# A sliding-window attention and gated-MLP kernel: the shape of its warm-up matmuls, the token parts of its first two tiles, and the places of its value-product runs

## Chip, cores and metric

The kernel runs on one core of a Trainium2 chip. The metric is the device time of one launch in microseconds. For the kernel before, three runs gave 557.01, 557.45 and 558.83 us, so the median is 557.45 us. One more run, with the profiler on, took 558.06 us; every duration in this document that comes from a row of the profile is from that run.

## What is computed

All matrices are bfloat16; there are 2048 tokens of 576 features.

```
xn = layernorm(x)                       # per token, no scale or shift
q, k, v = split(xn @ wqkv)              # 32 heads of 18
p = softmax(q k^T / sqrt(18))           # causal, a window of 256 tokens
s = concat(p v) @ wo
h = sigmoid(xn @ w_gate) * (xn @ w_up)  # 4608 wide
out = x + s * silu(h @ w_down)
```

## The kernel before

**Tiles.** The tokens are taken in four chunks of 512, each in four blocks of 128. The contraction over 576 features is five steps: four of 128 rows and one of 64 rows that is kept twice. `pair` (L119) issues every large matmul as two, on rows 0 to 63 and 64 to 127 of TensorE, which run beside each other. One such pair is four instructions of TensorE: two weight loads and two matmuls. A gate or up product of one 128-wide tile of the MLP is two such turns, `gate_up` (L991) with half 0 and half 1, of 512 tokens each; there are 36 tiles per chunk, then the down product `down` (L1075) with matmuls 288 wide.

**Order.** Nothing is ordered by hand. `build_graph` makes operations with estimates, priorities and dependences, and `schedule` (L1165) places them one after the other on a modelled clock, with attention work (scores, value products, output projection) laid between the MLP's tiles. `emit` then writes each engine's list with semaphore waits. A change in one place so moves the order of everything behind it.

**Value-product runs.** `build_pv` (L828) makes the products of the exponentials with the values for 16 heads at a time: two runs in each chunk, eight in all. A run is 128 small matmuls in the first chunk and 192 in the later ones, with as many weight loads, so 256 or 384 instructions that follow each other (row L854 of the profile). `schedule` does not start run number r before TensorE's list is at least `RUN_AT[r]` instructions long (L43, L1202). `at` counts weight loads, matmuls and an estimate of the waiting instructions.

**Start.** Layer norm of the first chunk runs block by block: statistics on VectorE (block 2 on ScalarE), the power by GpSimd (L555, L641), the scaling on VectorE (`ln:ap`, L563), the transposition on TensorE (`tr`, L650, four times two per block), the copy out of PSUM (`xe`, L631; ScalarE, for block 3 VectorE). The 64 rows that are kept twice are made apart: four small scalings on VectorE (`ln:dup`, L579, priority `DUP_PRIO`), one transposition for all blocks (`tr:two`) and one copy by ScalarE (`xe:two`). The first two MLP tiles (`NEARLY`) do not wait for all 512 tokens: `PARTS` (L76) cuts each turn over the four 128-row steps into token ranges, so that a range starts when its blocks' copies are done; `last_rows` (L1012) adds the fifth step for all tokens. Until the first block is there, `warm` (L496) issues matmuls of zeros: `NWARM` pairs, 43 before the first transposition and 10 behind it.

Of the kernel before, what the change touches and what calls it, by code (L numbers as in the profile page):

```python
# [12 lines left out]
P = 128  # L13
# [26 lines left out]
OENG = ("SP", "POOL")  # L40
PV_ORDER = (0, 5, -4, -3, -2, -1, 1, 2, 3, 4, 6, 7)
TURN_NS = 265.0
RUN_AT = (2138, 3723, 5614, 7169, 9467, 10942, 13309, 14840)  # L43
BINS = (((-4, 0, 1), (1, 1, 5), (6, 6, 2)),
        ((-2, 0, 3), (3, 3, 5)),
        ((0, 0, 5), (5, 5, 3)),
# [20 lines left out]
STATS_ACT = (2,)  # L67
APPLY_ACT = ()
ORDER = (("ln:ve:1", "ln:ap:0"), ("ln:ve:3", "ln:ap:2"), ("ln:am", "ln:rs:1"), ("ln:ve:3", "ln:dup:0"), ("ln:ve:3", "ln:dup:1"))
DUP_PRIO = 30  # L70
XE_ENG = ("ACT", "ACT", "ACT", "DVE", "ACT")
NWARM = (43, 10)
NEARLY = 2
FIRST_SLACK_NS = (-800.0, -1500.0)
BUSY_SLACK_NS = 1500.0
PARTS = (((0, 1), (1, 2), (2, 3), (3, 4)),) * NEARLY  # L76
NQK = 5

DMA_ISSUE_NS = {"SP": 640.0, "POOL": 520.0, "ACT": 650.0}
# [39 lines left out]
def pair(eng, outs, lhs, rhs, start, stop, swap=0, parts=False):  # L119
    res = None  # L120
    for i in range(2):
        t = i ^ swap
        res = eng.matmul(outs[i], lhs(ROWS[t], i), rhs(ROWS[t], i), start=start, stop=stop, tile_position=(64 * t, 0),  # L123
                         skip_group_check=parts)
    return res
# [137 lines left out]
class Builder:  # L263
# [17 lines left out]
    def op(self, eng, est, fn, name="", deps=(), prio=3, nbytes=0, odeps=(), acq=None, ni=0):  # L281
        o = Op(eng, est, fn, name, deps, prio, nbytes, odeps, acq)
        o.ni = ni
        assert ni or eng != "PE", name
        o.cidx = len(self.ops)
        self.ops.append(o)
        for d in o.deps:
            d.succs.append(o)
        for d in o.odeps:
            d.succs.append(o)  # L290
        return o
# [162 lines left out]
    def build_consts(self):  # L454
        op = self.op
        o1 = op("POOL", 200, lambda e: e.memset(self.ident[:, :], 0.0), "init:ident1", prio=0)
        o2 = op("POOL", 200, lambda e: e.affine_select(
            self.ident[:, :], self.ident[:, :], pattern=[[1, SW]], compare_op=ALU.not_equal, fill=1.0, base=0,
            channel_multiplier=-1), "init:ident2", deps=[o1], prio=0)
        self.op_ident = op("POOL", 200, lambda e: e.affine_select(  # L460
            self.ident[:, :], self.ident[:, :], pattern=[[1, SW]], compare_op=ALU.not_equal, fill=1.0, base=SW,
            channel_multiplier=-1), "init:ident3", deps=[o2], prio=0)
        zero = self.hT[:, 0, 0:P]
        z = op("DVE", 920, lambda e: e.memset(zero, 0.0), "init:zero", prio=0)
        self.op_negh = op("DVE", 60, lambda e: e.memset(self.neghalf[:, :], -0.5), "init:neghalf", prio=0)
        self.op_tab = op("ACT", 1500, lambda e: e.activation(self.tring[:, 0, 0:1], zero[:, 0:1], ACTF.Exp), "init:tab",
                         deps=[z], prio=0)
        self.warm_h = self.pool_f.hold()
        self.warm_src = zero
        self.warm(NWARM[0], z, None, 107)  # L470

    def load_wq(self, c, gi):
        sw, dw = self.r_wq.produce()
# [19 lines left out]
            o.slack = 5000.0 if c == 0 and name == "wv" else 2500.0  # L493
        return ds

    def warm(self, n, dep, before, est):  # L496
        h, zero = self.warm_h, self.warm_src

        def f_warm(eng):
            return pair(eng, self.halves(h, P), lambda r, t: zero[r, :],  # L500
                        lambda r, t: zero[r, :], True, True)
        for i in range(n):
            w = self.op("PE", est, f_warm, f"warm:{i}", deps=[dep], prio=4, acq=None if before else h, odeps=[before], ni=4)
            w.filler = h
            h.release(w)
            before = w

    def build_attn_consts(self):
        op = self.op
# [21 lines left out]
    def build_ln(self, c):  # L531
# [3 lines left out]
        for i in range(BPC):  # L535
# [40 lines left out]
            else:  # L576
                def f_two(e, mean=mean, rstd=rstd, x_in=x_in, i=i, op0=ALU.add if on_act else ALU.subtract):
                    row, col = x_in.ap
                    return e.tensor_scalar(self.xn2[:, i, :].rearrange("p (a c) -> p a c", a=2),  # L579
                                           bass.AP(x_in.tensor, x_in.offset, [row, (0, 2), (1, RD)]), mean, rstd, op0, ALU.mult)  # L580
                dup = op("DVE", 220, f_two, f"ln:dup:{st}", deps=[rs, ag], prio=DUP_PRIO)
                self.ln_dups.append(dup)
                self.r_st.release(ss, dup)
            self.r_st.release(ss, ap)
            if c:
                fl = self.flip(self.xnT[:, xs, :, i * P:(i + 1) * P], self.xnr[:, sn, :], f"flip:x:{st}", ("fx", xs, i),
                               deps=[dup, war], prio=2)
# [3 lines left out]
            h = self.pool_s.hold()  # L591
# [3 lines left out]
            tr = op("PE", (KB - 1) * 29.5, f_tr, f"tr:{st}", deps=[ap, self.op_ident, war], prio=0, acq=h, ni=4 * (KB - 1))  # L595
            self.r_xn.release(sn, tr)
            if i == 0:
                self.warm(NWARM[1], None, tr, 80)

            def f_xe(e, h=h, i=i):  # L600
                dst = self.xnT[:, xs, 1:KB, i * P:(i + 1) * P].rearrange("p k (t c) -> p t k c", t=2)
# [1 line left out]
            eng = XE_ENG[i]  # L603
            n = (KB - 1) * P
# [337 lines left out]
    def build_ffn(self, c):  # L942
# [48 lines left out]
        def gate_up(ft, h, half, acq, part=None, deps=(), behind=()):  # L991
            sw, fc = slots[ft // WG], slice((ft % WG) * P, (ft % WG + 1) * P)
            b0, b1 = (0, BPC) if part is None else PARTS[ft][part]
            t0, n = b0 * P, (b1 - b0) * P
            xin = (self.op_xnT[c] if part is None else self.op_x0)[b0:b1]

            def lhs(r, t, k):
                return self.wgs[r, sw, k - 1, t, fc] if k else self.wgr[r, rslots[ft // (2 * WG)], ft % (2 * WG) * P:(ft % (2 * WG) + 1) * P]

            def f(eng):  # L1000
                outs = [bank(h, w)[:, t0:t0 + n] for w in range(2)]
                if part is None:
                    return turn(eng, outs, lhs, lambda r, t, k: x_in[r, k, t0:t0 + n], half)
                return early_turn(eng, outs, lhs, lambda r, t, k: x_in[r, k, t0:t0 + n], half, part == 0)
            steps = len(BLOCKS[half] if part is None else BLOCKS[0])
            o = op("PE", steps * mm_ns(n), f, f"f1{half}:{c}:{ft}", deps=[xin, wops[ft // WG][0:1 + half if part is None else 1], deps],
                   prio=3 if part is None else 1, odeps=chain[half] if part is None else list(behind), acq=acq, ni=4 * steps)
            chain[half] = [o] if part is None else chain[half] + [o]
            self.ffn_last = o
            return o  # L1010
# [26 lines left out]
        if early:  # L1037
# [3 lines left out]
            for ft, h in enumerate(hs):  # L1041
                u = None
                for part in range(len(PARTS[ft])):
                    lo = gate_up(ft, h, 0, None if part else h, part, [u])
                    if ft == early - 1 and part == len(PARTS[ft]) - 1:
                        ahead = self.pool_f.hold()
# [118 lines left out]
    def schedule(self):  # L1165
# [19 lines left out]
        while nsched < len(ops):  # L1185
            best = None
            for e in ENGS:
# [10 lines left out]
                for o in cand:  # L1198
                    if e == "PE" and nxt is not None and o is not nxt:
                        continue  # L1200
                    st = max(free[e], ready_t[o.cidx])
                    if o.run and at < RUN_AT[runs]:  # L1202
                        continue
# [178 lines left out]
```

## Time and profile before

| | us |
|---|---|
| median of three runs | 557.45 |
| profiled run, whole | 558.06 |
| its span, first to last instruction | 556.8 |
| TensorE busy in it | 550.4 |
| VectorE, ScalarE, GpSimd busy | 324.5, 271.2, 208.6 |
| DMA, mean rate over the span | 136 GB/s |
| DMA, rate in the first 30 us | 237 GB/s |

A row of the timeline has the start in us, the time from the first start to the last end in us, the engine, the line, the operation, output and inputs with their shapes, and the count; brackets hold the idle time of the engine before it and what ended it. A matmul's end is modelled, and matmuls are pipelined: a matmul of 288 columns has a duration of 283 ns, yet a pair of them follows the last pair after some 119 ns. "Issue" is idle time for which the profile shows no semaphore. PEld are TensorE's weight loads. Waiting instructions are not counted in the views.

### The profile page before, as it was taken

How to read it: one execution, taken by the hardware profiler on the slowest of the kernel's cores; microseconds unless marked ns; L12 is line 12 of the kernel's file. 1: busy time of each engine (PE TensorE's matmuls, PEld its weight loads, DVE VectorE, ACT ScalarE, POOL GpSimd, SP SyncE). 2: the span in 40 equal slices, each digit the busy share in tenths (PEclk: the TensorE clock that was granted, in tenths of full speed). 3: DMA queues.
4: the chain of work that ended last, by engine and by line, in shares of the span. 5: the costliest groups of instructions: out<-in, count | busy, mean ns of one | idle time of the engine just before them, and what ended most of it. 6: DMA issues, size and time to landing. Idle time of an engine off the chain costs nothing.

```text
span 556.8 us, 19393 instructions
## 1 busy us (share of the span) xinstructions
PE 550.4 (99%) x8330; PEld 356.3 (64%) x8330; DVE 324.5 (58%) x782; ACT 271.2 (49%) x380; POOL 208.6 (37%) x360
## 2 busy tenths in 40 slices
PE   7999999999999999999999999999999999999998
PEld 7454445777756664468997555556778554445787
DVE  4467667756766558647546558556545477556211
ACT  4245563442565646653456626662556336762121
POOL 5634343846360333643730506542633305300300
PEclk9999999999999999999999999999999999999999
DMA  8999999442166673661153744754132246540010
GB/s 221 258 271 218 273 229 259 115 105 42 37 191 192 170 202 102 194 152 31 41 136 93 204 142 112 206 154 119 32 102 61 82 129 177 166 134 5 22 44 25
DMA packets 141213, 75.87 MB, mean 136 GB/s; under 512 B 43676, under 2 KB 139260, under 8 KB 141128
## 3 DMA queue, kind: packets, MB, share of 16 engines
q1 hardware_dynamic: 133704, 68.71, 46.6%
q0 software_dynamic: 7424, 5.92, 4.0%
q8 instruction: 66, 1.08, 0.8%
q14 instruction: 19, 0.16, 0.1%
HBM read 63.18 MB, written 2.36 MB: 118 GB/s over the span
## 4 chain that ended last, share of the span: by engine, by line
PE 98%; DMA 1%; issue 0%; SPq 0%; DVE 0%; ACT 0%
PE ps L123 95%; PE ps L854 3%; DMA wgs<-in_B_w_up_dram 1%; SPq L294 0%; PE ps L650 0%; ACT thf L1139 0%; DVE thf L1141 0%; DVE xf L1144 0%
## 5 line engine op out<-in xcount | busy, mean ns | idle before, releaser
L123 PE MATMUL ps<-xnT,wgs 64*128 64x512 bf16 (+1 forms) x2400 | 284.1, 368 | 0.4 <-DMA wgs<-in_B_w_up_dram 0.4
L804 ACT ACTIVATE expr<-ps 128x1024 bf16<-128x1024 f32 (+4 forms) x160 | 154.9, 968 | 77.5 <-PE ps L123 76.0
L123 PEld LDWEIGHTS ps<-xnT,wgs 64*128 64x128 bf16 x2400 | 119.8, 94 | 106.3 <-ACT xnT L631 0.5
L123 PE MATMUL ps<-wd_sb,hT 64*128 64x288 bf16 (+2 forms) x2448 | 155.9, 276 | 1.0 <-issue 0.8
L1025 ACT ACTIVATE tring<-ps 128x512 bf16<-128x512 f32 x144 | 86.2, 599 | 128.3 <-PE ps L123 127.4
L1028 DVE SCALAR_TENSOR_TENSOR hT<-tring,ps 128x512 bf16<-128x512 bf16 x144 | 98.7, 685 | 83.5 <-ACT tring L1025 81.5
L294 POOL DMA_DIRECT2D qk<-qd x160 | 82.7, 523 | 155.0 <-PE ps L123 148.5
L123 PEld LDWEIGHTS ps<-wd_sb,hT 64*128 64x128 bf16 x2448 | 117.8, 94 | 26.1 <-issue 1.6
L817 DVE TENSOR_TENSOR expr<-expr,mask 128x128 bf16<-128x128 bf16 (+2 forms) x240 | 63.9, 294 | 70.6 <-ACT expr L804 69.3
L294 POOL DMA_DIRECT2D oT<-o2T x72 | 36.8, 518 | 115.3 <-DVE o2T L890 71.6
L768 POOL TENSOR_SCALAR kx<-kprev,small 128x256 bf16<-128x256 bf16 x64 | 60.3, 952 | 5.6 <-PE ps L123 4.7
L123 PE MATMUL ps<-qk,kx 64*128 64x320 bf16 (+1 forms) x704 | 61.0, 254 | 0.0
L123 PE MATMUL ps<-xnT,wgr 64*128 64x512 bf16 x288 | 55.7, 376 | 0.0
L123 PEld LDWEIGHTS ps<-qk,kx 64*128 64x128 bf16 x704 | 34.7, 94 | 23.7
L123 PE MATMUL ps<-xnT,wqg 64*128 64x512 bf16 (+1 forms) x320 | 38.0, 355 | 0.0
L689 DVE CAST qd<-ps 128x1024 bf16<-128x1024 f32 (+1 forms) x20 | 22.3, 1115 | 7.7 <-PE ps L123 7.7
L123 PEld LDWEIGHTS ps<-xnT,wgr 64*128 64x128 bf16 x288 | 15.1, 94 | 15.8
L768 DVE TENSOR_SCALAR kx<-qk,small 128x512 bf16<-128x512 bf16 x64 | 21.7, 365 | 5.8 <-PE ps L123 5.5
L890 DVE STREAM_TRANSPOSE o2T<-o 128x512 bf16<-128x512 bf16 x32 | 22.6, 706 | 1.6 <-DMA oT<-o2T 1.1
L123 PEld LDWEIGHTS ps<-xnT,wqg 64*128 64x128 bf16 x320 | 15.9, 94 | 10.6 <-issue 0.4
L882 DVE STREAM_TRANSPOSE ot<-ps 128x512 f32<-128x512 f32 x32 | 20.1, 684 | 3.9 <-PE ps L854 3.9
L1141 DVE TENSOR_TENSOR thf<-thf,s_attn 128x576 bf16<-128x576 bf16 (+2 forms) x5 | 2.0, 398 | 31.4 <-ACT thf L1139 18.6
(71 smaller groups left out, 300.9 us busy)
## 6 DMA issues: line engine op xcount, KB each, us to landing
wgs<-in_B_w_gate_dram SPq DMA_DIRECT2D x72, 256.0 KB, 3.6
wgs<-in_B_w_up_dram SPq DMA_DIRECT2D x72, 256.0 KB, 4.1
wd_sb<-in_B_w_down_dram SPq DMA_DIRECT2D x9, 576.0 KB, 6.0
wqg<-in_A_wqkv_dram SPq DMA_DIRECT2D x32, 128.0 KB, 3.5
qk<-qd POOLq DMA_DIRECT2D x100, 36.0 KB, 2.4
wgr<-in_B_w_gate_dram SPq DMA_DIRECT2D x36, 64.0 KB, 2.5
wgr<-in_B_w_up_dram SPq DMA_DIRECT2D x36, 64.0 KB, 2.5
wvo<-in_A_wqkv_dram SPq DMA_DIRECT2D x4, 576.0 KB, 4.3
```

The costliest lines, as they stand in the source:

```text
L123: res = eng.matmul(outs[i], lhs(ROWS[t], i), rhs(ROWS[t], i), start=start, stop=stop, tile_position=(64 * t, 0), skip_group_check=parts)
L294: o = self.op(eng, DMA_ISSUE_NS[eng], lambda e: e.dma_start(dst, src), name, deps, prio, nbytes=nbytes)
L689: return eng.tensor_copy(dst, self.both(h, n))
L768: return e.tensor_scalar(self.kx[:, sx, pos:pos + n_ // SW, t, :], src.rearrange("p (s k) -> p s k", k=SW), self.half[:, t:t + 1], None, A ...
L804: return eng.activation(self.expr[:, se, :, lo * SW:NT], self.both(h, NT)[:, :, lo * SW:NT], ACTF.Exp, scale=SM_SCALE)
L817: return eng.tensor_tensor(e_, e_, m_, ALU.mult)
L854: res = eng.matmul(outs[i][p0:p0 + VH, cols], self.v_aug[ROWS[i], o:o + VH], self.expr[ROWS[i], se, t, cols], start=m == 0, stop=m == len( ...
L882: return e.transpose(self.ot1[:, p1, :], self.halves(hp, NT, un)[i])
L890: t2 = op("DVE", dve_ns(NT), lambda e, p2=p2, p3=p3: e.transpose(self.o2T[:, p3, :], self.o2[:, p2, :]), f"ot2:{c}:{pr}:{i}", deps=[on, d3 ...
L1025: th = op("ACT", act_ns(NT), lambda e: e.activation(self.tring[:, st, :], bank(h, 0), ACTF.Tanh, scale=0.5), f"th:{c}:{ft}", deps=[pg, dt_ ...
L1028: mu = op("DVE", dve_ns(NT), lambda e: e.scalar_tensor_tensor(self.hT[:, ft, :], self.tring[:, st, :], 1.0, bank(h, 1), ALU.add, ALU.mult) ...
L1141: q2 = op("DVE", dve_ns(w, 2.0), lambda e: e.tensor_tensor(t, t, s_, ALU.mult), f"fq2:{nm}", deps=[th, self.op_s[sb]], prio=0)
```

## The change

Four constants and `warm` change.

- `RUN_AT`: the eight least places of the value-product runs.
- `WARM` takes the place of `NWARM`: groups of (width, estimate, count). Before the first transposition there are 9 pairs of 512 columns and 7 of 128 in place of 43 of 128, behind it 5 pairs of 256 in place of 10 of 128. The wide ones read the same 128 zero columns two or four times over.
- `PARTS`: blocks 0, 1 and (2, 3) in place of 0, 1, 2, 3, in both early tiles: three token ranges in place of four.
- `DUP_PRIO` goes from 30 to 14.

```diff
-RUN_AT = (2138, 3723, 5614, 7169, 9467, 10942, 13309, 14840)
+RUN_AT = (2079, 3886, 5846, 7648, 9681, 11466, 13541, 15054)
...
-DUP_PRIO = 30
+DUP_PRIO = 14
...
-NWARM = (43, 10)
+WARM = (((512, 427, 9), (128, 107, 7)), ((256, 160, 5),))
...
-PARTS = (((0, 1), (1, 2), (2, 3), (3, 4)),) * NEARLY
+PARTS = (((0, 1), (1, 2), (2, 4)),) * NEARLY
...
-        self.warm(NWARM[0], z, None, 107)
+        self.warm(WARM[0], z, None)
...
-    def warm(self, n, dep, before, est):
+    def warm(self, groups, dep, before):
         h, zero = self.warm_h, self.warm_src
-
-        def f_warm(eng):
-            return pair(eng, self.halves(h, P), lambda r, t: zero[r, :],
-                        lambda r, t: zero[r, :], True, True)
-        for i in range(n):
-            w = self.op("PE", est, f_warm, f"warm:{i}", deps=[dep], prio=4, acq=None if before else h, odeps=[before], ni=4)
-            w.filler = h
-            h.release(w)
-            before = w
+        for n, est, count in groups:
+            def f_warm(eng, n=n):
+                return pair(eng, self.halves(h, n), lambda r, t: zero[r, :],
+                            lambda r, t: zero[r, :][:, None, :].broadcast_to([64, n // P, P]), True, True)
+            for i in range(count):
+                w = self.op("PE", est, f_warm, f"warm:{n}:{i}", deps=[dep], prio=4, acq=None if before else h, odeps=[before], ni=4)
+                w.filler = h
+                h.release(w)
+                before = w
...
-                self.warm(NWARM[1], None, tr, 80)
+                self.warm(WARM[1], None, tr)
```

In the two built programs, counted in TensorE's own order with its waiting instructions: the list is 16,924 instructions long before and 16,733 after. The eight runs start at instruction 2139, 3724, 5625, 7170, 9481, 10968, 13320 and 14858 before, and at 2095, 3902, 5853, 7649, 9693, 11479, 13549 and 15063 after. Between the first two MLP tiles and the first run the order of TensorE's matmuls is the same; from the first run on, runs and other attention work stand elsewhere among the MLP's. On VectorE one of the four `ln:dup` moves ahead of the last `ln:ap`, and the copy `xe` of block 3 moves behind all four. SyncE's first fifteen rows of transfers are the same; behind them weight loads of the MLP come earlier against those of q and k.

## The prediction, made before the changed kernel was run

> **What bounds the kernel now.** The page first: span and busy time.
>
> ```profile
> span 556.8 us, 19393 instructions
> PE 550.4 (99%) x8330; PEld 356.3 (64%) x8330; DVE 324.5 (58%) x782; ACT 271.2 (49%) x380; POOL 208.6 (37%) x360
> q8 instruction: 66, 1.08, 0.8%
> ```
>
> TensorE is busy all the time and no other engine is near it, so only two things count: the work on TensorE, and the few places where it stands still. The view of waits, for TensorE alone, names those:
>
> ```profile
> PE ps L123 <- DVE small L465: 1.1, 1, 1.1
> PE ps L650 <- issue: 1.0, 1, 1.0
> PE ps L123 <- issue: 0.8, 1, 0.8
> PE ps L650 <- DVE xnr L563: 0.5, 2, 0.3
> PE ps L123 <- DMA wgs<-in_B_w_up_dram: 0.4, 1, 0.4
> ```
>
> Three are the start: until the zeros are there, until the first blocks are scaled, until the first weights have landed. The two "issue" rows wait for no semaphore. The chain of waits places them and shows a third:
>
> ```profile
> 10.41 0.97 issue
> ...
> 138.83 0.83 issue
> ...
> 387.40 0.13 issue
> ```
>
> What are they? Windows laid from one such place to the next, with DMA's instruction queue in the same windows:
>
> ```profile
> 11.38:139.65 128.27, 127.45 (x1759) 74.07 (x1759) 81.79 (x217) 57.00 (x87) 64.07 (x106) 1.00 0.80 197
> 139.66:387.52 247.86, 247.74 (x3646) 163.83 (x3645) 156.51 (x359) 134.91 (x183) 98.98 (x168) 1.00 0.51 139
> ```
>
> ```profile
> q8 instruction: 14, 0.23, 0.8%
> ...
> q8 instruction: 29, 0.48, 0.8%
> ```
>
> The page's 66 packets carry 1.08 MB, 16.4 KB each: 256 instructions of 64 B. In the built order, waiting instructions included, the first matmul after each of the three gaps is number 449, 4033 and 11457: exactly 14 and 29 times 256 apart, as the 14 and 29 packets say (3,518 and 7,291 matmuls and weight loads, the rest waits). So TensorE stops where a block of its own instructions has not arrived. I call numbers 193 + 256 n edges. A packet starts after each edge, once DMA lets it: the rows below are for 5.84 to 8.94 and 8.94 to 11.37 us, 135.6 to 137.2 and 137.2 to 139.65, 383.1 to 385.1 and 385.1 to 387.5.
>
> ```profile
> q1 hardware_dynamic: 1551, 0.85, 98.0%
> ...
> q8 instruction: 1, 0.02, 3.1%
> ...
> q1 hardware_dynamic: 1125, 0.14, 55.9%
> ...
> q8 instruction: 1, 0.02, 2.3%
> ...
> q1 hardware_dynamic: 910, 0.46, 81.1%
> ...
> q8 instruction: 1, 0.02, 2.4%
> ```
>
> Before each gap, bulk transfers fill the queue and the fetch comes after them. The block that is fetched from one edge on is needed at the next, and the time between two edges is short only where small instructions run fast:
>
> ```profile
> 135.27 1.86 PE L854 MATMUL ps<-expr,v_aug 64*19 64x320 bf16 x128
> 137.06 1.77 PE L123 MATMUL ps<-wd_sb,hT 64*128 64x288 bf16 x26
> 139.66 1.03 PE L123 MATMUL ps<-wd_sb,hT 64*128 64x288 bf16 x14 [0.83 <-issue]
> ...
> 381.79 2.47 PE L854 MATMUL ps<-expr,v_aug 64*19 64x320 bf16 x192
> 384.19 2.62 PE L123 MATMUL ps<-wd_sb,hT 64*128 64x288 bf16 x40
> 386.65 0.39 PE L123 MATMUL ps<-qk,kx 64*128 64x64 bf16 x6
> ```
>
> In a run, 192 matmuls and 192 loads take 2.40 us (381.79 to 384.19): 6.3 ns an instruction. The last edge before 4033 lies 53 instructions into the run, at 135.6, so its block took 4.0 us to arrive (139.66). Before 11457 it lies 233 into the run, at 383.2: 4.3 us. But the edge before that one stands 23 instructions ahead of the run, at some 380.8, and its block was there at 383.2 with no gap in the row: 2.4 us or less.
>
> **The sum.** I start from the profiled run's 558.06 us (its span and 1.25 around it), 0.61 above the median.
>
> *The start.* These are TensorE's rows:
>
> ```profile
> 7.61 0.62 PE L123 MATMUL ps<-xnT,wgs 64*128 64x128 bf16 x16 [0.42 <-DMA wgs<-in_B_w_up_dram]
> 8.05 0.30 PE L650 MATMUL ps<-ident,xnr 64*128 64x64 bf16 x8
> ...
> 8.73 1.64 PE L123 MATMUL ps<-xnT,wgs 64*128 64x128 bf16 x48
> 10.19 0.22 PE L650 MATMUL ps<-ident,xn 64*128 64x64 bf16 x3
> 11.38 0.24 PE L650 MATMUL ps<-ident,xn 64*128 64x64 bf16 x5 [0.97 <-issue]
> 11.45 1.32 PE L123 MATMUL ps<-xnT,wgs 64*128 64x128 bf16 x40
> 12.61 0.38 PE L123 MATMUL ps<-xnT,wgr 64*128 64x512 bf16 x2
> ...
> 15.21 2.75 PE L123 MATMUL ps<-xnT,wgs 64*128 64x512 bf16 x24
> ```
>
> Nothing changes up to 7.61, where weights end the wait and their transfers keep their places. The warm-up's 53 pairs become 21: 128 instructions fewer; the parts become 96 matmuls for 128: 64 fewer. So edge 193, passed at about 5.9 before, falls among the 24 matmuls between the transpositions of blocks 2 and 3, at about 8.5, and edge 449 among the 512-wide ones at about 16. That leaves 7.5 us; the block that made the gap came 5.4 after its edge (5.95 to 11.38) with DMA at 98%. The gap goes. It is worth 1.14: the fourth transposition would have started at 10.24, 50 ns after the first.
>
> The parts: 40 matmuls 128 wide take 1.16 (11.45 to 12.61), 58 ns a pair. A pair 512 wide takes 215 (16 more in 15.21's row than in a row of 8, 2.75 against 1.03), so a 256-wide one is put at 109, between them. 32 pairs at 58 become 16 at 109: 0.11 less. Block 3's copy is now needed for the wide part, and VectorE makes it last:
>
> ```profile
> 8.95 0.42 DVE L631 COPY xnT<-ps 128x512 bf16<-128x512 bf16 x1 [0.22 <-PE ps L650]
> 9.29 0.75 DVE L579 TENSOR_SCALAR xn<-x,small 128x128 bf16<-128x128 bf16 x3
> ```
>
> Behind three scalings of 0.25 it ends at about 9.7 in place of 9.37. TensorE has 64 matmuls 128 wide (29 ns each) and three transpositions (0.12) to do from 7.61, until 9.8. It is covered by 0.1; without that cover it costs its lateness, at most 0.3. Taken at 0. The twice-kept rows are needed later, at 11.1; their copy is earlier than before. The last weights of that tile (wgr) must land by 11.1 too, and not by 12.6; taken at 0.
>
> The warm-up rows:
>
> ```profile
> 1.05 4.53 PE L123 MATMUL ps<-hT 64*128 64x128 bf16 x86 [1.05 <-DVE small L465]
> 5.97 0.72 PE L123 MATMUL ps<-hT 64*128 64x128 bf16 x20
> ```
>
> [...] 9 pairs of four times 105 and 7 of 105 fill 4.5 us, as now, and 5 of 109 fill 0.55. [...]
>
> *The runs.* An idle row understates a stop: a matmul of 283 ns is followed after 59. So 0.83 and 0.13 are worth 0.16 more each: 0.99 and 0.29, 1.28 together. In the built order the second run now ends 130 instructions ahead of an edge, not 53, with the last edge 131 instructions after its start: over 5 us. The first is like it. Those two and their 1.28 go.
>
> The new places of the other six are what costs. They start 28, 32, 28, 22, 44 and 22 instructions behind an edge, where before five of six started 56 to 73 behind one, and the one at 381.79 23. With 54 ns an instruction for 512-wide pairs, 30 for 288-wide (59 a matmul) and 6.3 in the run, the time from that edge to the one in the run is 2.95, 2.37, 2.95, 2.13, 3.71 and 2.13 us. From there to the next it is 3.9 for the fourth run, 4.1 for the sixth and eighth, over 5 for the others. Bounds: if each block comes within 2.1, as the 2.4 at 380.8 lets one hope, 0. If each takes the 4.0 of 135.6, and behind the runs the 4.3 of 383.2: 1.05 + 1.63 + 1.05 + 1.87 + 0.29 + 1.87, and 0.4 + 0.2 + 0.2: 8.6. The nearest row is the one at 380.8, an edge 23 ahead of a run, without a stop. But 512-wide matmuls stood before it; before the fourth, sixth and eighth run stand 288-wide ones, so TensorE's queue, filled ahead, gives less time. I take 0 for the others and a fifth of 1.63 + 1.87 + 1.87 for those three: 1.1.
>
> *Else.* Both programs hold the same matmuls outside the start, and the views show no other wait of TensorE in 546 us. In the new order the last chunk's second run stands 400 instructions nearer the end, and the last x loads follow later stores; 2.9 us median to landing by the view of that tile, hidden behind ten us of matmuls. Taken at 0.1.
>
> ```profile
> DMA to landing us min/median/max: 1.5/2.9/5.5
> ```
>
> Sum: 558.06 - 1.14 - 0.11 - 1.28 + 1.1 + 0.1 = 556.7; less 0.61, **556.1 us** against the median.
>
> [...]
>
> **The rivals.**
>
> 1. *All fetches come in time*: no run stops. For: 380.8. Against: DMA's bursts come as they like. 556.1 - 1.1 = 555.0.
> 2. *The new edges stop every run* (the other side). The fetch of the edge just ahead of a run comes behind a burst of loads, as at 135.6 and 383.2, and the run has to wait in its middle. It decides from about 4.4 us of stops in all, 0.7 a run; at the upper end it is 8.6: 555.0 + 8.6 = 563.6. For: intervals of 2.1 to 3.0 where 3.2 (4.02 less its stop) was too short. Against: the edge lies before the run, where TensorE has a queue to work off, and 380.8.
> 3. *The gaps aren't fetches*, or the place of the runs does not matter: only the parts' 0.11 is had: 557.3. Against: 14 and 29 packets.
> [...]
>
> **How the numbers follow.** Stops of 0.2 to 2.2 us (my forecast): 0.62, giving 555.2 to 557.2. Rival 1: 0.16. Stops of 2.2 to 4.1, short of rival 2: 0.08. Rival 2: 0.07. Rivals 3 and 4: 0.07. A measurement here tells 0.3%, 1.67 us, from no change: 555.8 to 559.1. Faster needs under 0.8 us of stops: rival 1 and a little over a third of my own case, 0.40. Slower: rival 2 and a little of the others, 0.08. Same: 0.52. The range leaves out two in ten: half of rival 1's better end, rival 2 and the worse end of the case beside it: 554.7 to 558.2.
>
> **What would show it.** Right: no idle row near 10 us, and the 24 matmuls of 15.21 start 1.2 to 1.3 earlier; no gap behind the second run; TensorE's idle rows of "issue" lie in the value-product runs, 190 to 240 instructions after their start, those of the fourth, sixth and eighth first. Wrong: a gap within 12 us of the start (the fetch of edge 193 took over 7 us), an idle row that waits for ScalarE or VectorE in the reordered middle, or stops over 1 us in more than two runs.

## The result and the profile after

The changed kernel takes 556.61 us (median of 22 runs, 555.21 to 558.36), the kernel before beside it 557.99 us (22 runs, 556.59 to 561.83); the ratio is 0.9973, 95% interval 0.9962 to 0.9985. That is 1.5 us faster in the ratio, and 0.5 us slower than the 556.1 forecast. The forecast stood 1.35 below 557.45, the median of three runs; the two medians here differ by 1.38, so the 0.5 is the kernel before, which takes 0.54 more in these runs. The profiled run of the changed kernel took 557.37 us, 0.8 above its median, with a span of 556.1. In the experiments below one run, at 638.96 us and a granted clock of 0.851 where all others had 0.996 to 1.000, is left out of its kernel's ratio.

The page of the changed kernel, the rows that answer to those of before:

```profile
span 556.1 us, 19203 instructions
PE 550.5 (99%) x8234; PEld 342.4 (62%) x8234; DVE 323.9 (58%) x782; ACT 272.1 (49%) x380; POOL 208.8 (38%) x360
q8 instruction: 65, 1.06, 0.8%
```

96 matmuls and 96 loads fewer, one fetch packet less, TensorE as busy as before. Its waits in the changed kernel (engine and tile, what ended the wait, us in all, times, longest):

```profile
PE ps L123 <- DVE small L465: 1.0, 1, 1.0
PE ps L123 <- DMA wgs<-in_B_w_up_dram: 0.3, 1, 0.3
PE ps L123 <- DMA wd_sb<-in_B_w_down_dram: 1.4, 1, 1.4
```

Both "issue" rows of before are gone: in this trace TensorE waits for no block of its instructions. In their place stands a wait that before did not have, for a transfer of down weights. The timeline of TensorE shows the start without the gap, the new wait behind the first run, and the sixth run:

```profile
7.48 0.62 PE L123 MATMUL ps<-xnT,wgs 64*128 64x128 bf16 x16 [0.33 <-DMA wgs<-in_B_w_up_dram]
...
9.68 1.71 PE L123 MATMUL ps<-xnT,wgs 64*128 64x128 bf16 x32
...
14.03 2.77 PE L123 MATMUL ps<-xnT,wgs 64*128 64x512 bf16 x24
...
94.68 1.86 PE L854 MATMUL ps<-expr,v_aug 64*19 64x320 bf16 x128
...
100.82 0.33 PE L123 MATMUL ps<-qk,kx 64*128 64x320 bf16 x4
102.58 2.13 PE L123 MATMUL ps<-wd_sb,hT 64*128 64x288 bf16 x32 [1.44 <-DMA wd_sb<-in_B_w_down_dram]
...
402.77 2.47 PE L854 MATMUL ps<-expr,v_aug 64*19 64x320 bf16 x192
405.17 2.62 PE L123 MATMUL ps<-wd_sb,hT 64*128 64x288 bf16 x40
```

No idle time stands before the row at 9.68, and the 24 matmuls that started at 15.21 start at 14.03: 1.18 earlier. TensorE's own end moved from 554.32 to 553.44 by the two chains of waits, 0.88 earlier. This is 1.18 for the start and 1.28 for the two old stops, less 1.60 for the new wait (1.44 idle and the 0.16 by which an idle row understates a stop): 0.86. For these two traces the account closes.

The chain of waits of the changed kernel names what is late at 102.58:

```profile
95.66 6.88 DMA wd_sb<-in_B_w_down_dram
```

This is the last of the nine down-weight loads of the first chunk; it lands 6.88 us after its issue. SyncE's timeline says where it stands in the queue, in the kernel before and then in the changed one:

```profile
92.48 0.53 SPq L294 DMA_DIRECT2D xnr<-in_A_x_dram  x1
93.06 0.47 SPq L294 DMA_DIRECT2D wd_sb<-in_B_w_down_dram  x1
```

```profile
93.93 0.59 SPq L294 DMA_DIRECT2D wgs<-in_B_w_gate_dram  x1
94.56 0.51 SPq L294 DMA_DIRECT2D wgs<-in_B_w_up_dram  x1
95.17 0.45 SPq L294 DMA_DIRECT2D xnr<-in_A_x_dram  x1
95.66 0.47 SPq L294 DMA_DIRECT2D wd_sb<-in_B_w_down_dram  x1
```

In the built queue a gate and an up load now stand ahead of it that stood behind it before, and it is issued 2.6 us later. The queue alone holds it back: the product of VectorE that it has to wait for was done at 87.25. It is also needed sooner. The first product that uses it started at 102.39 before, and would start here at 101.0 without the wait (102.58 less 1.60); 1.2 of these 1.4 us are the start's own gain.

### The profile page after: what moved, and what is told of

It is laid out like the page before. It is cut to its first block, busy times and chain, and to the rows that moved or that the text cites. A ratio compares the mean times of both kernels' runs of the same rounds, so it can differ in the third digit from the quotient of the medians.

```text
span 556.1 us, 19203 instructions
## 1 busy us (share of the span) xinstructions
PE 550.5 (99%) x8234; PEld 342.4 (62%) x8234; DVE 323.9 (58%) x782; ACT 272.1 (49%) x380; POOL 208.8 (38%) x360
## 4 chain that ended last, share of the span: by engine, by line
PE 97%; DMA 2%; SPq 0%; ACT 0%; DVE 0%; issue 0%
PE ps L123 94%; PE ps L854 3%; DMA wd_sb<-in_B_w_down_dram 1%; DMA wgs<-in_B_w_up_dram 1%; SPq L294 0%; ACT tring L1025 0%; PE ps L650 0%; ACT thf L1139 0%; DVE thf L1141 0%; DVE xf L1144 0%; DVE hT L1028 0%
## 5 line engine op out<-in xcount | busy, mean ns | idle before, releaser
L123 PE MATMUL ps<-xnT,wgs 64*128 64x512 bf16 (+2 forms) x2368 | 283.7, 370 | 0.4 <-DMA wgs<-in_B_w_up_dram 0.3
L123 PEld LDWEIGHTS ps<-xnT,wgs 64*128 64x128 bf16 x2368 | 117.0, 94 | 107.5 <-ACT expr L804 0.5
L123 PE MATMUL ps<-wd_sb,hT 64*128 64x288 bf16 (+2 forms) x2448 | 153.8, 276 | 1.4 <-DMA wd_sb<-in_B_w_down_dram 1.4
L123 PEld LDWEIGHTS ps<-wd_sb,hT 64*128 64x128 bf16 x2448 | 112.7, 94 | 31.2 <-DMA wd_sb<-in_B_w_down_dram 1.7
L123 PE MATMUL ps<-qk,kx 64*128 64x320 bf16 (+1 forms) x704 | 59.4, 254 | 0.0
L123 PEld LDWEIGHTS ps<-qk,kx 64*128 64x128 bf16 x704 | 32.2, 94 | 24.4
L936 ACT ACTIVATE s_attn<-ps 128x576 bf16<-128x576 f32 x16 | 10.2, 650 | 23.0 <-PE ps L123 22.9
```

Of the source, the lines that this page charges most:

```text
L936: return eng.activation(dst, self.both(h2, 288), ACTF.Copy, scale=1.0 if c == NC - 1 else 0.25)
```

## The experiments

**My theory**: the gain is the fetch stop at the start (1.14) and those behind the second and the sixth run (1.28), and part of it is given back in a wait for down weights that the later first run causes. **Rivals**: places against block borders are worth nothing and the gain is the start's, or the parts', alone; the wait is an accident of one execution. A border is what the prediction calls an edge, instruction 193 + 256 n of TensorE's built list, counted from 0. Its time is the start of that instruction in the trace, found by counting, and a packet's time is that of its record in DMA's instruction queue.

### Borders moved, all else equal

```diff
-RUN_AT = (2079, 3886, 5846, 7648, 9681, 11466, 13541, 15054)
+RUN_AT = (2163, 3970, 5930, 7732, 9765, 11550, 13625, 15138)
-WARM = (((512, 427, 9), (128, 107, 7)), ((256, 160, 5),))
+WARM = (((512, 427, 2), (128, 107, 35)), ((256, 160, 5),))
```

> The changed kernel with 42 more, narrower warm-up matmuls of about the same length, and the same order of all else: every later instruction's number is 84 higher, so the block borders fall 0 to 22 instructions behind the ends of the third to eighth run and 61 and 46 behind the first two. Fetch theory: six stops of 1.0 to 2.0 us just behind those runs, near 232, 279, 352, 406, 475 and 523 us, and perhaps 0.8 behind the second: 562 to 567 us. Rival, places do not matter and gaps are something else: 556.6, no idle rows of issue at those places.

Measured: 566.94 us (4 runs), ratio to before 1.0160 (1.0140 to 1.0180). Its waits and the "issue" rows of its chain:

```profile
PE ps L123 <- issue: 9.2, 7, 1.9
```

```profile
98.53 1.88 issue
...
231.07 1.74 issue
...
531.46 0.81 issue
```

Seven stops: six just behind the third to eighth run, as expected, and one behind the first, which I had not listed. The second run has none. They sum to 9.2 idle and, with 0.16 each, 10.3 us. Its profiled run took 566.14: the 557.37 of the changed kernel, less the 1.60 for down weights, which this trace does not have, and with these 10.3 make 566.1. Beside the warm-up the lists of all engines are the same in the two built programs, so places against borders are what counts, and the rival falls.

### The warm-up's count undone

```diff
-WARM = (((512, 427, 9), (128, 107, 7)), ((256, 160, 5),))
+WARM = (((128, 107, 43),), ((128, 80, 10),))
-RUN_AT = (2079, 3886, 5846, 7648, 9681, 11466, 13541, 15054)
+RUN_AT = (2207, 4014, 5974, 7776, 9809, 11594, 13669, 15182)
```

> The changed kernel with the 53 narrow warm-up pairs of the kernel before (128 instructions more; all later instructions and the runs' numbers 128 higher); blocks 2 and 3 stay together. Fetch theory with what the traces gave so far (a block is of use 1.4 us behind its packet's end): at the start the second border's block is there at about 11.4 and needed at about 10.4: a stop of 0.7 to 1.3 us near 10.4, so that the fewer warm-up instructions, not the wider parts, took the start's stop away. Each of the last six runs now holds two borders 256 run instructions, 1.6 us, apart: a stop of 1.5 to 2.2 us inside each, 28 instructions ahead of its end; the first two runs end 17 and 2 ahead of a border: 0.5 to 1.9 each. In all 566 to 571 us. Rival, the start's gain was the parts': no idle row near 10.4. Rival, places don't matter: 556.6.

Measured: 571.35 us (one run). Its timeline has the start's stop back and a stop inside the third run:

```profile
11.16 0.93 PE L123 MATMUL ps<-xnT,wgs 64*128 64x256 bf16 x13 [0.49 <-issue]
...
228.84 2.39 PE L854 MATMUL ps<-expr,v_aug 64*19 64x320 bf16 x178
234.09 0.27 PE L854 MATMUL ps<-expr,v_aug 64*19 64x128 bf16 x14 [2.87 <-issue]
```

```profile
PE ps L854 <- issue: 11.5, 6, 2.9
PE ps L123 <- issue: 2.1, 3, 1.1
```

178 of the third run's 192 matmuls, then 2.87 us of nothing, then the last 14, which are 28 instructions: the place that the borders give. Six such stops sum to 11.5, three others to 2.1. In all it is just above the 566 to 571 expected. At the start the idle row is 0.49, not 0.7 to 1.3: TensorE got there at 10.68 and not at 10.4, and the block came at 11.16 and not at 11.4. Beside the warm-up the lists of all engines are those of the changed kernel, and the parts are still wide: they alone do not take the start's stop away.

### The parts undone

```diff
-PARTS = (((0, 1), (1, 2), (2, 4)),) * NEARLY
+PARTS = (((0, 1), (1, 2), (2, 3), (3, 4)),) * NEARLY
-RUN_AT = (2079, 3886, 5846, 7648, 9681, 11466, 13541, 15054)
+RUN_AT = (2143, 3950, 5910, 7712, 9745, 11530, 13605, 15118)
```

> The changed kernel with blocks 2 and 3 of the first two tiles taken singly again (64 instructions more, all later borders and runs' numbers moved with them, so that the ends of the third to eighth run stand 20 to 42 instructions ahead of a border, and 64 to 108 instructions from the border before to the run's start). Theory: the first border's block was there at 14.2 us in the changed kernel and is needed here at about 12.7: a stop of 1 to 1.7 us near 12.7, so the wider parts were needed, too, for the start's gain; and stops of 0.5 to 1.2 us behind each of the six later runs: 560 to 564 us. Rival, the fewer warm-up matmuls alone removed the start's stop: no idle row near 12.7. Rival, places don't matter: 556.7.

Measured: 562.35 us (4 runs), ratio 1.0078 (1.0057 to 1.0099). Rows of its timeline at the start, and at the third run:

```profile
11.74 1.25 PE L123 MATMUL ps<-xnT,wgs 64*128 64x512 bf16 x16
12.83 0.38 PE L123 MATMUL ps<-xnT,wgr 64*128 64x512 bf16 x2
...
232.30 1.02 PE L123 MATMUL ps<-xnT,wgs 64*128 64x512 bf16 x7 [0.53 <-issue]
```

No idle row at 12.8: I expected a stop of 1 to 1.7 there and was wrong, because the first border's packet came at 10.41 to 11.37 in this run and not at 11.60 to 12.81 as in the changed kernel's first trace. The block was needed at 12.81, 1.44 after its packet's end, and blocks that TensorE stopped for were used 1.25 to 1.57 after theirs (last section). So in this one trace the fewer warm-up instructions alone removed the stop, with nothing to spare, and the parts add cover: in the two traces of the changed kernel the same block is needed 3.2 and 4.2 us behind its packet. The later stops came where they were expected, 0.17 to 0.56 idle each and so at the small end, with one of 1.09 behind the first run that I had not listed.

### The runs alone, on the kernel before

```diff
-RUN_AT = (2138, 3723, 5614, 7169, 9467, 10942, 13309, 14840)
+RUN_AT = (2138, 4142, 6090, 7880, 9937, 11722, 13797, 15310)
```

> The kernel before with its start as it was, its first run in its old place, and the other seven put at places against the block borders that give no stop in the changed kernel's trace or, for the fourth run, in the trace of before (116, 21, 64, 20, 22, 37, 22 instructions behind a border). Fetch theory: the start's 0.97 us of issue stays, those of 0.83 and 0.13 behind the second and sixth run go, and the down-weight wait of the changed kernel is not there, because the first run stands where it did: 558.0 - 1.28 = 556.7 us. Rival, the gain was the start's alone: 558.0.

Measured: 562.59 us (6 runs), ratio 1.0080 (1.0062 to 1.0098): 5.9 above the forecast. Rows of its chain of waits:

```profile
10.85 0.68 issue
...
232.13 0.17 issue
...
476.60 0.23 issue
...
553.89 3.32 DMA xf<-in_A_x_dram
```

The down-weight wait is not there, the start's stop is, and the old stops behind the second and sixth run are gone, as expected. Two things are otherwise. The end: TensorE's last row there starts at 552.82 and lasts 2.49, so it ends at 555.3, but the span ends at 561.2; 5.9 lie behind TensorE, where before had 2.5. The last x loads wait for stores of the output, and these for the last run: by the chain, a store issued at 550.70 lands 3.17 later and releases the load at 553.89. And TensorE itself ends 1.0 later than before, not 1.28 earlier. Its waits hold two new fetch stops inside runs (0.17 and 0.23 idle) and three waits of 0.13 to 0.16 for TensorE's own earlier work just behind runs; with the 0.16 by which each of these rows understates, and 0.15 more at the start, this is 1.8 of the 2.3. The other 0.5 I could not find. So the time of this kernel decides nothing between the two sides: its trace shows that moved runs lose the old stops, and that they can get others.

For the first of the two stops the row of DMA's main queue suggests why, in two windows of this kernel ahead of the third run's packet (228.0 to 229.2, 229.2 to 229.9) and then in one of the changed kernel (224.5 to 225.1):

```profile
q1 hardware_dynamic: 630, 0.31, 89.5%
...
q1 hardware_dynamic: 388, 0.19, 92.2%
```

```profile
q1 hardware_dynamic: 74, 0.06, 36.6%
```

Here the border, 21 instructions ahead of the run, is passed at 229.18 in a burst, and its packet starts at 229.97. In the changed kernel a border 28 ahead is passed at 225.72 and its packet had started at 225.17. That is one pair of windows; the last section has packets that came late with DMA idle.

### The last run alone later

```diff
-RUN_AT = (2079, 3886, 5846, 7648, 9681, 11466, 13541, 15054)
+RUN_AT = (2079, 3886, 5846, 7648, 9681, 11466, 13541, 15310)
```

> The changed kernel with the last value-product run alone 256 instructions later in the work, so at the same distance from its block borders. Fetch theory: no stop. Theory that the last x loads, which follow the stores behind that run, have little cover left: in the changed kernel they were issued at 547.96, landed by about 552 and were used at 553.5 to 554; 256 instructions later, by 6 to 8 us, they land at 557 to 560 and the end comes 3 to 6 us later with TensorE's own end unmoved: 559.5 to 562.5 us. Rival, the tail of the kernel with the seven moved runs came from something else and these loads have ten us of cover, as the prediction took it: 556.6.

Measured: 562.34 us (4 runs), ratio 1.0074 (1.0049 to 1.0098). SyncE's last rows, of the changed kernel and then of this one:

```profile
546.03 1.22 SPq L294 DMA_DIRECT2D out_dram<-xf  x2
547.96 2.13 SPq L294 DMA_DIRECT2D xf<-in_A_x_dram  x2
553.45 1.33 SPq L294 DMA_DIRECT2D out_dram<-xf  x3
```

```profile
552.21 1.22 SPq L294 DMA_DIRECT2D out_dram<-xf  x2
553.99 1.23 SPq L294 DMA_DIRECT2D xf<-in_A_x_dram  x2
558.45 1.32 SPq L294 DMA_DIRECT2D out_dram<-xf  x3
```

TensorE's last row ends at 553.75, 0.3 behind the changed kernel's, and the end comes 4.9 us later: first stores 6.2 later, x loads 6.0, last stores 5.0. Behind the moved run itself there is no stop; one of 0.37 stands at 547.6, where the last instructions now lie otherwise. This settles the tail of the kernel with the seven moved runs, whose last run also stands later in the work than the changed kernel's.

### The second run alone put back

```diff
-RUN_AT = (2079, 3886, 5846, 7648, 9681, 11466, 13541, 15054)
+RUN_AT = (2079, 3710, 5846, 7680, 9681, 11466, 13541, 15054)
```

> The changed kernel with the second value-product run alone put back to where it stood against the block borders before (202 instructions behind one, its end 54 ahead of the next); the fourth run then falls 112 behind a border with its end 16 ahead of the next; the other six stay. Fetch theory: an idle row of issue behind the second run, worth 0.8 to 1.1 us, and one just behind the fourth run, worth 1.0 to 2.0 (its block is asked for 241 instructions before its need, some 2.2 us, and comes after 3.4 to 4.2): 558.4 to 559.7 us. Rival, places of runs are worth nothing and the gain over the kernel before came from the start and the wider parts alone: 556.6.

Measured: 558.02 us (12 runs, 556.88 to 562.96), ratio to before 1.0007 (0.9985 to 1.0029). The profiled execution, 556.93, is one of its fastest. Rows of its chain:

```profile
143.84 0.14 issue
...
279.41 0.95 issue
```

The fourth run's stop is there, 0.95 and 0.16. At the second run I was wrong: there is no fetch stop. The 0.14 is a wait for TensorE's own earlier work, as TensorE's timeline says:

```profile
142.79 1.03 PE L123 MATMUL ps<-xnT,wgs 64*128 64x512 bf16 x8
143.98 1.04 PE L123 MATMUL ps<-xnT,wgs 64*128 64x512 bf16 x8 [0.16 <-PE ps L123]
```

The distances are those of before, but 512-wide matmuls stand behind the run now, so the next border comes 3.9 us after the one inside the run (140.25, 144.11), where it came after 3.2 plus the stop; and the packet started 0.9 behind that border (141.15) where before it started 1.6 behind (135.64, 137.21). In these two traces the place made a stop possible; the widths of the matmuls around it and the time at which the packet started made it one. The wide scatter of this kernel's times fits that, but only one of its executions has a trace.

### The first run alone put back

```diff
-RUN_AT = (2079, 3886, 5846, 7648, 9681, 11466, 13541, 15054)
+RUN_AT = (1946, 3886, 5846, 7648, 9681, 11466, 13541, 15054)
```

> The changed kernel with the first value-product run alone put back to where it stood in the work before, 219 instructions behind a block border with its end 36 ahead of the next; the others as they are, 2 instructions later. Theory that the later first run made the down-weight wait: no row that waits for wd_sb, down products again from about 98; but behind the run, near 92, a stop of 0 to 1.2 us, because its block is asked for 255 instructions, some 3.2 us, before its need and such blocks took 3.2 to 4.4. So 555.0 to 556.4 us. Rival, the wait is independent of the first run's place: 556.6 and the row again.

Measured: 557.93 us (12 runs), ratio 1.0005 (0.9992 to 1.0017). Its timeline:

```profile
86.48 1.86 PE L854 MATMUL ps<-expr,v_aug 64*19 64x320 bf16 x128
88.28 2.12 PE L123 MATMUL ps<-xnT,wgs 64*128 64x512 bf16 x17
92.34 1.02 PE L123 MATMUL ps<-xnT,wgs 64*128 64x512 bf16 x7 [1.95 <-issue]
```

No row waits for wd_sb. But the stop behind the run is 1.95, more than the 0 to 1.2 expected: the packet started 3 us behind the border (86.71, 89.75), among the loads of the first chunk. The stop also delays the down products, so it hides part of what was asked. But the gate and up loads are behind the down-weight load again, which is issued at 91.32; with 6.88 more it lands at 98.2, and without the stop it would be needed at 100.9 (103.00 less 2.1). By this estimate there is no wait either. The first run's new place costs a wait sometimes; its old place, with the borders that the new start gives, costs a larger stop.

### The down weights earlier, in two ways, and the changed kernel once more

```diff
# let go after tile 26 of gate and up, not 30
-deps=[hm[min(fg * FG + 2 - fg // 2, 31)]], prio=6))
+deps=[hm[min(fg * FG + 2 - fg // 2, 31 if fg < 8 else 26)]], prio=6))
# or: a better priority for the last load
+deps=[hm[min(fg * FG + 2 - fg // 2, 31)]], prio=6 if fg < 8 else 1))
```

> The last down-weight load of each chunk is let go after tile 26 of gate and up instead of tile 30, so in chunk 0 it stands nine loads earlier in SyncE's queue; TensorE's order is that of the changed kernel. If the 1.44 us wait at 102.58 is a standing part of the changed kernel's time and is worth 1.60 with the shadow of the matmul behind it: 555.0 us (1.6 under the changed kernel), and no row of TensorE that waits for wd_sb. If that wait was one of the profiled execution only, or if the loads now behind it come late in its place: 556.6, no change, in the second case with rows that wait for wgs or wgr near 94 to 98 us.

> The changed kernel with the last down-weight load given a better priority in the plan (eight loads earlier in SyncE's queue, behind the same tile of gate and up); TensorE's order unchanged. Theory that this load is what is late: 555.0 to 555.9 us, no row that waits for wd_sb, the same as with the earlier let-go (555.81). If the gate and up loads behind it come late instead: 556.6 and rows that wait for wgs or wgr between 94 and 100 us.

> The same as the kernel with the last down-weight load eight loads earlier, once more, for more executions: if it is better than the changed kernel, 555.4 to 556.0 us again and no wait for wd_sb; if the 0.5 us between the two was chance, 556.2 to 556.6.

> The changed kernel once more, for a second trace. If the 1.44 us wait for wd_sb at 102.58 is a standing part: again a row of 1 to 2 us there, SyncE's issue of that load after 95, 556.6 us, and 0.8 to 1.6 us behind the kernels that load it earlier. If it comes and goes with how far SyncE is behind (95.66 in the one trace, 93.84 and 92.98 in two kernels with the same order up to there, without the wait): no such row, issue before 94.5, and a time of executions scattered between 555.0 and 556.8. No stop of issue in either.

| | median us | runs | ratio to before, 95% |
|---|---|---|---|
| changed kernel | 556.61 | 22 | 0.9973 (0.9962 to 0.9985) |
| changed kernel again | 556.31 | 12 | 0.9972 (0.9961 to 0.9984) |
| load let go after tile 26 | 555.81 | 6 | 0.9955 (0.9938 to 0.9973) |
| load with better priority | 555.75 | 7 | 0.9963 (0.9949 to 0.9977) |
| the same again | 555.80 | 9 | 0.9955 (0.9939 to 0.9972) |

The second trace of the changed kernel has no wait for wd_sb; SyncE issued that load at 93.62, not 95.66. It has a stop at nearly the same place, where I had expected none:

```profile
101.40 0.34 PE L123 MATMUL ps<-qk,kx 64*128 64x320 bf16 x4 [0.33 <-issue]
```

There the packet of the border passed at 95.71 started at 98.91 and its block was used at 101.40, 5.7 us behind the border. The account closes for this trace, too: the 24 matmuls start at 14.12, 1.09 earlier than before, the two old stops are gone, and this stop costs 0.49. That makes 1.88, and TensorE's end, at 552.40, is 1.92 earlier. The kernels with the load earlier have neither; the timeline of the one with the better priority:

```profile
100.95 0.33 PE L123 MATMUL ps<-qk,kx 64*128 64x320 bf16 x4
101.11 2.12 PE L123 MATMUL ps<-wd_sb,hT 64*128 64x288 bf16 x32
```

So the 1.44 is not a standing wait. It comes and goes with how far behind SyncE is: of the traces with this queue and no stop just ahead of the load's first use, the one with the issue at 95.66 waits, and those at 94.50 and 93.84 do not. Both sides were partly right: three measurements at 555.75 to 555.81 against 556.31 and 556.61, 0.5 to 0.9 us and not the 1.6 I had expected. Each interval alone overlaps that of the changed kernel; together they lean to a gain. This is the best version found. Whether the 0.5 to 0.9 is the wait, the small stop or both can't be told from single traces.

## Why the prediction was right, and where its steps were off

- **What the gaps are.** Right, and now shown by moving only the numbers of the instructions: seven stops of 0.66 to 1.88 where borders fall behind runs, six of 11.5 in all where two borders fall into one run. Two readings of mine were off. Number 11457 is a weight load, and the first matmul there is the next instruction. And a packet need not start behind its edge: for the row at 380.8 that I leaned on, the edge was passed at 380.84 and the packet had started at 379.88, and over the whole trace of before packets start from 1.2 us ahead of their edge (253.05, 251.82) to 3.3 behind (332.94, 336.22). TensorE passes all 65 borders of the changed kernel without a stop in its first trace, and all but one in its second; at borders just behind a run it stops, as the 9.2 us of issue in the kernel with moved borders say.
- **The start, 1.14 and 0.11.** Right in sum: 1.18 measured at the 24 matmuls, 0.13 of it from weights that landed earlier (7.48 against 7.61), so 1.05 of the 1.25; no idle row at 10. That is less than the gap's 1.14 alone, so no run shows the 0.11 of the parts. In the second trace it is 1.09: the first real matmuls start earlier still, at 7.31, and a row of 0.28 at 8.21 waits for VectorE's scaling of block 2. Block 3's copy ends at 9.76, as forecast, and nothing waits for it. I had counted the instructions of warm-up and parts together; in the one trace that tests it the warm-up's were just enough. `DUP_PRIO` was not tried alone.
- **The warm-up's pace.** Before, the pairs of the row at 1.05 took 105 ns each in the mean (4.53 us for 43), those of the row at 5.97 took 56 (0.72 less 0.22 for the last matmul, nine steps). Right that the wide ones cost nothing behind them: the first 16 matmuls behind the weights take 0.62 us at 7.48, as they did at 7.61. The fourth rival, that the slow pace lasts past 7.61, falls. What changes the pace no run shows: in both kernels the view by windows gives a granted clock of 1.00 from 0 to 5.20 us and from there to the first weights' matmuls alike.
- **The stops behind the second and sixth run, 1.28.** Right in sum: neither stop is in either trace of the changed kernel. The reason, longer distances, is only half shown, and over 5 us was not safe everywhere: at the first run, of which I had said the same, the second trace has a stop 5.7 us behind its border. And with the second run's old distances there was no stop either, in other surroundings. The sixth keeps its distances, 22 behind a border in place of 23 and its end 106 ahead of the next in place of 105. Its stop went because the packet came sooner: border 404.10, packet 404.98 to 405.91, with no other transfer between the two, where before had 383.16 and 385.19 in a burst. Nothing in my step would have told me that.
- **New stops in the fourth, sixth and eighth run, 1.1.** Failed: 0. I had bounded the arrival by 2.1 and 4.0 us and leaned a fifth of the way up, because 288-wide matmuls, at 119 ns a pair against 215 for 512-wide ones, give TensorE's queue less time. The packets show that the border ahead of a run is asked for up to 0.73 us before TensorE passes it, while wide matmuls are still being worked off:

| run, changed kernel | border passed by TensorE | packet | block needed |
|---|---|---|---|
| fourth | 274.29 | 274.30 to 275.24 | 276.66 |
| sixth | 401.94 | 401.21 to 402.09 | 404.10 |
| eighth | 519.46 | 518.79 to 519.74 | 521.62 |

  A packet so starts between 0.7 ahead of TensorE and level with it, and with some 1.4 us from packet to use there are 0 to 0.6 us of cover. The first rival was right in this term. It was close: the fourth had none left, and in the kernel before with moved runs such stops did come, 0.17 and 0.23 idle, the first with DMA at 90%.
- **Else, 0.1.** Failed in two of its parts. "No other wait of TensorE" overlooked the first run: I followed its borders but not what its move does to SyncE's queue. The last down-weight load comes to stand behind two more loads, is issued up to 2.6 us later and is needed 1.4 us sooner, so it has no cover left: 1.60 in one trace. The 0.49 of the other trace is a fetch behind the same run. And the last x loads are not hidden behind ten us of matmuls. VectorE already waited for the first of them in the changed kernel, as two rows of VectorE's timeline say:

```profile
550.65 0.46 DVE L1144 TENSOR_TENSOR xf<-xf,thf 128x576 bf16<-128x576 bf16 x1 [2.59 <-DMA xf<-in_A_x_dram]
552.72 0.37 DVE L1141 TENSOR_TENSOR thf<-thf,s_attn 128x416 bf16<-128x416 bf16 x1 [1.61 <-ACT thf L1139]
```

  The next operation still waits 1.61 for ScalarE, so about 1.6 us of cover are left, and 256 instructions more, 6 us, cost 4.9. It cost nothing here, but by 1.6 us and not by ten.

By the profiled runs, the forecast's terms were -1.14, -0.11, -1.28, +1.1, +0.1; measured were -1.18 for the first two, -1.28, 0 and +1.60 in the first trace, and -1.09, -1.28, 0 and +0.49 in the second. The two main gains were forecast rightly, but that the total came so near is luck: 1.1 of stops that did not come stood against a wait or a stop of 0.5 to 1.6 that I had not seen.

## What to carry to other kernels

Where TensorE runs hundreds of tiny instructions in a few microseconds, count its instructions: 384 took 2.40 us in a run. Every run here holds a border, and that alone costs nothing. In the changed kernel the later runs have one border 22 to 44 instructions ahead of them, the next inside, and the one behind that 84 to 106 past their end: no stop, though before the sixth run had one of 0.13 at just these distances. With a border 0 to 22 behind the end of a run, so soon after the one inside, 0.66 to 1.74 us were lost, and with two borders inside a run 1.4 to 2.9. Any edit that changes the number of instructions ahead of it moves all the borders behind it (84 more in the warm-up made seven stops, 9.2 us idle), so tune the places last and look at every run of the new trace. When a block of work is moved, look at the queues of transfers as well: loads and stores near it change places or come later, and lose their cover, at the run's new place (1.44 idle for down weights) and at the end of the program (4.9 us with the last run later) alike.

## What the runs showed that was not expected

- From the end of a packet to the first use of its block no stop took less than 1.25 or more than 1.57 us, over 33 stops in nine traces: close to a fixed time behind the transfer. Packets are 0.9 to 1.8 us long, so what varies most is when one starts: from 1.7 us ahead of TensorE's passing the border (335.65, 334.00 in the changed kernel) to 3.7 behind (189.28, 193.01 in the kernel with the second run put back).
- A border inside a run had its packet behind TensorE even with DMA idle: 0.8 us at 408.87 in the kernel with moved borders, whose queue rows for 408.9 to 409.6 are empty, and for 409.6 to 410.7 are

```profile
q8 instruction: 1, 0.02, 5.6%
```

  With no other transfer in between it was 1.6 at 403.90 in the kernel with the second run put back, and 2.9 at 359.63 in the kernel with the warm-up's count undone, just behind a stop. So a full queue is not all that makes a packet late; nor were the queues ahead of the three packets of before equally full, with 98, 56 and 81% in the prediction's rows. What else decides it stays open.

- The same order of issues ran up to 2.7 us apart in SyncE: the last down-weight load was issued at 95.66, 94.50, 94.03, 93.84, 93.62 and 92.98 in six traces with the same queue up to it. A cover of 2 us for such a load would not be sure here.
